# Agent attention and a SoLU feed-forward: the square of u without a bias column

## The chip, the cores and the metric

The kernel runs on one core of one Trainium2 chip. The metric is the device time of one execution in microseconds. Engines are named as in the profile: PE multiplies matrices (PEld loads its stationary operand), DVE is VectorE, ACT is ScalarE, POOL is GpSimd, SP issues the DMAs. Each runs its own list of instructions in order and waits on semaphores for the others.

## The reference, cut to what matters

```python
s = scale * (agents @ k.T); a2k = softmax(s); agent_v = a2k @ v
x = softmax(scale * (q @ agents.T)) @ agent_v       # 4 x 12608 tokens of 128
h = x @ w_in                                        # 128 -> 1024
e = exp(h - max(h)); sm = e / (sum(e) + 1e-9)
solu = h * sm
mu, var = mean(solu), mean((solu - mu) ** 2)
ln = (solu - mu) / sqrt(var + 1e-6) * g_ln
out = ln @ w_out                                    # 1024 -> 128
```

The kernel takes the mean of each column out of the scaled `w_out` beforehand, so the token's own mean is needed in the variance alone. It works with u = h * exp(h - max), not yet divided by the sum S of the exponentials; S then enters as a term that is added to the variance before the reciprocal root.

## The kernel before, in words

A tile is 128 tokens; there are 394. Each goes through the same steps.

- `c_h`: PE writes h into one of two PSUM buffers (`ph`).
- `c_max`: DVE writes -h and its row minimum to SBUF (`e_a`, `e_b`).
- `c_exp`: ACT writes the exponential back over `ph`, with the minimum as its bias column, and accumulates S.
- `c_u`: DVE multiplies the two into u (one of six buffers), and its accumulator gives the sum of u, in one of eight small tiles `su`.
- `c_sq`: ACT squares u. The function gets `-1024*u + su`, where `su` is the instruction's bias column, so the row sum of what it writes is the centred sum of squares, kept in a column of `Q`. The tile `sq` that it writes is read by nobody.
- For 11 of 13 tiles, `c_f0` and `c_f1` split u into two 16-bit parts (POOL, some of the first parts on ACT), `c_x` turns them by a transposing DMA, and `c_w` makes 24 matmuls. For the others PE transposes u itself (`c_t`, `c_ev`) and `c_w` makes 8 matmuls in fp32.

After a group of 16 tiles (8 at the ends, 2 in the last) `c_rstd` computes the reciprocal roots for the group: `t0` on ACT, `r2` on POOL (`t = Q + t`), two ACT functions (`y`), then four small POOL instructions up to `yc`. `c_fin` on DVE scales four tiles' results by `yc` on their way out of PSUM.

Between these lie the attention's first half for the next batch (`phase_a`) and the softmax over the agents for eight tiles at a time (`phase_b`).

The order of all instructions on all engines is written out beforehand: `STEPS` (lines 25 to 151) is a packed list of operations, and `Plan.run` issues them in that order. What stands in `op(...)` as a cost only decides which PSUM bank an operation takes.

Of the kernel before, what the change touches and what calls it, by code (L numbers as in the profile page):

```python
# [13 lines left out]
F32 = mybir.dt.float32  # L14
# [4 lines left out]
AF = mybir.ActivationFunctionType  # L19
ALU = mybir.AluOpType  # L20
# [146 lines left out]
class Plan:  # L167
# [17 lines left out]
    def op(self, eng, fn, cost, due, deps=(), take=False, free=None, after=(), kind=1, shy=0.0):  # L185
        o = Op()
        o.kind, o.shy = kind, shy
        o.eng, o.fn, o.cost, o.due, o.take, o.free = eng, fn, cost, due, take, free
        o.deps, o.outs, o.end, o.bank = [d for d in deps if d is not None], [], None, None
        o.left = 0  # L190
        self.ops.append(o)
        for d in o.deps + [d for d in after if d is not None]:
            if d.end is None:
                o.left += 1
                d.outs.append(o)
        return o
# [39 lines left out]
def kernel(  # L236
# [11 lines left out]
    nc = tc.nc  # L248
    B, C, N = kT.shape
    A = agT.shape[2]  # L250
    DF = w_in.shape[1]
    P = 128
# [3 lines left out]
    RT = 16  # L256
# [12 lines left out]
    UBUF = 6  # L269
# [73 lines left out]
    engs = (mybir.EngineType.PE, mybir.EngineType.Activation, mybir.EngineType.DVE, mybir.EngineType.Pool, mybir.EngineType.SP)  # L343
    SCALE = 1.0 / math.sqrt(C)
    INV = 1.0 / DF
    LIFT = DF ** 1.5

    const = ctx.enter_context(tc.tile_pool(name="const", bufs=1))
    mpool = ctx.enter_context(tc.tile_pool(name="mpool", bufs=2))
# [2 lines left out]
    tiny = ctx.enter_context(tc.tile_pool(name="tiny", bufs=4))  # L352
# [5 lines left out]
    ident = const.tile([P, P], F32, name="ident")  # L358
# [58 lines left out]
    def ring(m, shape, dt, name):  # L417
        return [const.tile(shape, dt, name=f"{name}_{chr(97 + i)}") for i in range(m)]

    pad = const.tile([P, 8], F32, name="pad")  # L420
    er, ur = ring(2, [P, DF], F32, "e"), ring(UBUF, [P, DF], F32, "u")
# [23 lines left out]
    def conv_out():  # L445
# [52 lines left out]
        def spread_ev():  # L498
            nc.vector.tensor_copy(out=wsc, in_=pm[0][:, :2])
            for i, k in enumerate((-0.5 * LIFT, 1.5 * LIFT)):  # L500
                nc.vector.tensor_scalar(out=lif[:, i : i + 1], in0=pm[0][:, 1:2], scalar1=k, scalar2=None, op0=ALU.mult)
# [39 lines left out]
    op = plan.op  # L541
# [11 lines left out]
    rgrp = {}  # L553
# [4 lines left out]
    def both(x):  # L558
        return seq[x][0] % 2 == 1 and seq[x][1] == 0

    sur, fcr = ring(8, [P, 1], F32, "su"), ring(12, [P, 1], F32, "fc")
    mxr, smr = ring(4, [P, UB], F32, "mx"), ring(4, [P, UB], F32, "sm")
    mdone, mlast, last_h, ex, CB, cbs = {}, {}, {}, {}, {}, {}
    bmats = {}
# [1 line left out]
    def phase_a(b, due, gate):  # L566
# [166 lines left out]
        def q5():  # L733
            cb, r = cbs[b], res["pr"]
            ri = r.bitcast(I32)
            nc.vector.tensor_scalar(out=ri[:, 1:2], in0=ri[:, 2:3], scalar1=0x7F800000, scalar2=None, op0=ALU.bitwise_and)
            k = math.sqrt(1e-6 * DF) * DF
            for i, z, f in ((1, 0, 2.0 ** 13 * k), (2, 0, 2.0 ** 13 * k * 1e-9), (3, 1, -(2.0 ** -14)), (4, 0, -(2.0 ** 13))):
                nc.vector.tensor_scalar(out=cb[:, i : i + 1], in0=r[:, z : z + 1], scalar1=float(f), scalar2=None, op0=ALU.mult)

# [40 lines left out]
        for c in range(NC):  # L781
# [3 lines left out]
            z = c * 2.55  # L785
# [16 lines left out]
        z = NC * 2.55 - (8.0 if head else 1.5)  # L802
# [10 lines left out]
        z = NC * 2.55 + 1.0  # L813
        fa = op("P", f1, 0.24, at(z), [AC[NCK], o7], take=True)
        fb = op(ETE, f2, (0.16, 0.2), at(z + 0.2), [fa] + mdone.get(b - 1, []))
        fc = op("D", q1, 0.2, at(z + 0.2), [fa], free=fa, after=[fb])
        fd = op("P", q2, 0.3, at(z + 0.4), [fc, wmax], take=True)
        fe = op("D", q3, 0.22, at(z + 0.5), [fd, OLD_CB.get(b - 2)], free=fd)
        CB[b] = op("D", q5, 0.33, at(z + 0.9), [fe])
        mdone[b] = []  # L820
        f4 = None
# [122 lines left out]
    us, phs, nms, nhs, rr, pr, st, fs, rs_ = {}, {}, {}, {}, {}, {}, {}, {}, {}  # L944
# [14 lines left out]
    def scal(x):  # L959
        return cbm[x] if both(x) else cbs[seq[x][0]]  # L960
# [25 lines left out]
    def c_exp(x):  # L986
        R, j = rgrp[x]
        if R not in rs_:
            rs_[R] = {z: tiny.tile([P, RT], F32, tag=z, name=f"{z}{R}") for z in "SQ"}
        nc.scalar.activation(out=phs[x], in_=nhs[x], func=AF.Exp, scale=-1.0, bias=nms[x], accum_out=rs_[R]["S"][:, j : j + 1])  # L990

    def xbar(x):
        return x % PEN not in PEP and x < n - TD

    def c_u(x):
        us[x] = (ur[x % UBUF], sur[x % 8])
        u, su = us[x]
        nc.vector.scalar_tensor_tensor(out=u, in0=nhs[x], scalar=scal(x)[:, 4:5], in1=phs[x],  # L998
                                       op0=ALU.mult, op1=ALU.mult, accum_out=su)

    def c_f0(x, k="G"):
        f = fs[x] = fr_[fl.index(x) % FBUF]
        if k == "A":
            nc.scalar.copy(out=f[:, 0, :], in_=us[x][0])
        else:
            nc.gpsimd.tensor_scalar(out=f[:, 0, :], in0=us[x][0], scalar1=1.0, scalar2=0.0, op0=ALU.mult, op1=ALU.add)

    def c_f1(x):
        nc.gpsimd.tensor_tensor(out=fs[x][:, 1, :], in0=us[x][0], in1=fs[x][:, 0, :], op=ALU.subtract)

    def c_x(x):
        pr[x] = xr[fl.index(x) % XB]
# [1 line left out]

    def c_sq(x):
        R, j = rgrp[x]
        u, su = us[x]
        sq = sqr[x % 2]
        nc.scalar.activation(out=sq, in_=u, func=AF.Square, bias=su, scale=-float(DF),  # L1019
                             accum_out=rs_[R]["Q"][:, j : j + 1])  # L1020

    def c_t(x, hf, pt):
        rr[x, hf] = pt
        for kf in range(4):
            k0 = hf * 4 + kf
            nc.tensor.transpose(pt[:, kf * P : (kf + 1) * P], us[x][0][:, k0 * P : (k0 + 1) * P], ident)  # L1026

    def c_ev(x, hf, k="A"):
        if hf == 0:
# [4 lines left out]
    def c_w(x, m0, m1, px=None):  # L1034
        G, j = divmod(x, GT)
        if px is not None:
            st[G] = {"po": px}
        po, t = st[G]["po"][:, j * P : (j + 1) * P], pr[x]
        mm = []
        for kf in range(NF):  # L1040
            if xbar(x):
                mm += [(t[:, kf, :], wh16, kf), (t[:, kf, :], wl16, kf), (t[:, NF + kf, :], wh16, kf)]
            else:
                mm.append((t[:, kf, :], w32, kf))
        for q in range(m0, m1):
            ut, wt, kf = mm[q]
            nc.tensor.matmul(po, ut, wt[:, kf, :], start=(q == 0), stop=(q == len(mm) - 1))  # L1047

    def c_rstd(R, m):
        gp = nc.gpsimd  # L1050

        def g(z):
            return rs_[R][z][:, :m]

        def t0():
            for z in ("t", "y", "z", "yc"):
                rs_[R][z] = tiny.tile([P, RT], F32, tag=z, name=f"{z}{R}")
            j0 = 0
            while j0 < m:
                c = scal(RS0[R] + j0)  # L1060
                j1 = next((j for j in range(j0, m) if scal(RS0[R] + j) is not c), m)
                nc.scalar.activation(out=rs_[R]["t"][:, j0:j1], in_=rs_[R]["S"][:, j0:j1], func=AF.Square,
                                     scale=c[:, 1:2], bias=c[:, 2:3])
                j0 = j1

        def r2():
            gp.tensor_tensor(out=g("t"), in0=g("Q"), in1=g("t"), op=ALU.add)

        def r3(z):
            if z == 0:  # L1070
                nc.scalar.activation(out=g("y"), in_=g("t"), func=AF.Ln, scale=float(2.0 ** -64))
            else:
                nc.scalar.activation(out=g("y"), in_=g("y"), func=AF.Exp, scale=-0.5, bias=lnb)

        def r4():
            gp.tensor_tensor(out=g("z"), in0=g("y"), in1=g("y"), op=ALU.mult)

        def r5():
            gp.tensor_tensor(out=g("z"), in0=g("z"), in1=g("t"), op=ALU.mult)

        def r6():
            gp.tensor_scalar(out=g("z"), in0=g("z"), scalar1=lif[:, :1], scalar2=lif[:, 1:2], op0=ALU.mult, op1=ALU.add)

        def r7():
            gp.tensor_tensor(out=g("yc"), in0=g("y"), in1=g("z"), op=ALU.mult)

        return t0, (("G", r2, 0.17), ("A", lambda: r3(0), 0.19), ("A", lambda: r3(1), 0.23), ("G", r4, 0.2), ("G", r5, 0.24), ("G", r6, 0.39), ("G", r7, 0.18))


# [10 lines left out]
    def F(f, *x):  # L1100
        return lambda *y: f(*x, *y)
# [45 lines left out]
    def at(x, d, r, l):  # L1147
        return x + d + (r * (1.0 - x / 12.0) if x < 12 else l if x >= X0[B - 1] else 0.0)

    H, MX, EX, U, SQ, T, EV, W, FIN, F0, F1, XT = ({} for _ in range(12))  # L1150
# [3 lines left out]
    for x in range(n):  # L1154
        b, t = seq[x]
        G, j = divmod(x, GT)
# [18 lines left out]
        used = [T.get((x - UBUF, 0)), T.get((x - UBUF, 1)), SQ.get(x - UBUF), F1.get(x - UBUF)]  # L1175
        U[x] = op("D", F(c_u, x), 1.205, at(x, DU_ + (0.0 if xbar(x) else DUF), DUR, DUL), [EX[x], CB[b]] + used + (cin if x < 2 else cout if x < UBUF else []), after=[U.get(x - 1)])
        SQ[x] = op("A", F(c_sq, x), 1.14, at(x, DSQ + (0.0 if xbar(x) else DSQF), DSQR, DSQL), [U[x]] + ([om] if not x else []))
        if xbar(x):
            fl.append(x)
# [20 lines left out]
        for m0 in range(0, num, step):  # L1200
            m1 = min(m0 + step, num)
            lead = m0 == 0 and j == 0
            f = (lambda px, x=x, m1=m1: c_w(x, 0, m1, px)) if lead else F(c_w, x, m0, m1)
# [93 lines left out]
```

## Time and profile before

| what | value |
| --- | --- |
| time, median of 3 runs | 1253.42 us (1252.56 to 1254.7) |
| span of the profiled execution | 1258.3 us |
| busy: PE, DVE, ACT, POOL | 97%, 95%, 94%, 89% of the span |
| squares of u on ACT (line 1019) | 394 |
| `r2` on POOL (line 1067) | 27 |

The profile gives the span of one execution, from the first to the last instruction, and no separate time for that execution; the span is 4.9 us over the median of the timed runs. Busy shares of four engines lie close together, so a single share names no bound: what decides is which engine is idle in which stretch, and for whom it waits. An ACT instruction with an accumulator shows as two rows, the function and a short ACTIVATION_READ_ACCUMULATOR.

### The profile page before, as it was taken

How to read it: one execution, taken by the hardware profiler on the slowest of the kernel's cores; microseconds unless marked ns; L12 is line 12 of the kernel's file. 1: busy time of each engine (PE TensorE's matmuls, PEld its weight loads, DVE VectorE, ACT ScalarE, POOL GpSimd, SP SyncE). 2: the span in 40 equal slices, each digit the busy share in tenths (PEclk: the TensorE clock that was granted, in tenths of full speed). 3: DMA queues.
4: the chain of work that ended last, by engine and by line, in shares of the span. 5: the costliest groups of instructions: out<-in, count | busy, mean ns of one | idle time of the engine just before them, and what ended most of it. 6: DMA issues, size and time to landing. Idle time of an engine off the chain costs nothing.

```text
span 1258.3 us, 36373 instructions
## 1 busy us (share of the span) xinstructions
PE 1214.6 (97%) x14304; PEld 936.6 (74%) x14304; DVE 1200.0 (95%) x2292; ACT 1183.8 (94%) x2212; POOL 1119.7 (89%) x889
## 2 busy tenths in 40 slices
PE   7989999999999999999999999999999999999998
PEld 4567777777777877777878777777787777777778
DVE  5799999999999999999999999899999999999997
ACT  5599999999999999999999999899999999999998
POOL 3488898999999898889999989789899999999995
PEclk8989999999999999999999999999999999999999
DMA  9599999999999999999999999999999899898896
GB/s 368 199 204 237 230 243 234 236 234 216 197 203 237 246 227 245 254 265 234 214 209 208 249 227 224 225 248 252 224 227 195 167 202 216 168 230 199 194 190 169
DMA packets 721516, 281.41 MB, mean 224 GB/s; under 512 B 692672, under 2 KB 696256, under 8 KB 721344
## 3 DMA queue, kind: packets, MB, share of 16 engines
q1 hardware_dynamic: 721344, 279.08, 103.2%
q8 instruction: 112, 1.84, 0.6%
q14 instruction: 60, 0.49, 0.1%
HBM read 79.67 MB, written 25.82 MB: 84 GB/s over the span
## 4 chain that ended last, share of the span: by engine, by line
ACT 24%; PE 24%; DVE 21%; issue 14%; POOL 9%; DMA 6%; SPq 0%; POOLq 0%; DVEq 0%; ACTq 0%
ACT ph L990 10%; PE px L1047 10%; PE ph L955 7%; ACT sq_b L1019 5%; ACT sq_a L1019 5%; DVE e_b L983 5%; DVE e_a L983 4%; PE px L654 2%; PE px L601 2%; DVE u_c L998 2%; DVE u_d L998 2%; DVE u_e L998 1%; DVE u_a L998 1%; PE px L1026 1%; DVE u_b L998 1%
## 5 line engine op out<-in xcount | busy, mean ns | idle before, releaser
L983 DVE TENSOR_SCALAR_CACHE_REDUCE e_a<-ph,nk 128x1024 f32<-128x1024 f32 x197 | 251.5, 1277 | 10.1 <-PE ph L955 9.2
L983 DVE TENSOR_SCALAR_CACHE_REDUCE e_b<-ph,nk 128x1024 f32<-128x1024 f32 x197 | 251.6, 1277 | 5.5 <-PE ph L955 5.0
L990 ACT ACTIVATE ph<-e_a,nm 128x1024 f32<-128x1024 f32 x197 | 219.3, 1113 | 16.3 <-DVE e_a L983 14.7
L990 ACT ACTIVATE ph<-e_b,nm 128x1024 f32<-128x1024 f32 x197 | 219.3, 1113 | 9.6 <-DVE e_b L983 8.4
L998 DVE SCALAR_TENSOR_TENSOR u_d<-e_b,cb,ph 128x1024 f32<-128x1024 f32 x66 | 84.2, 1276 | 2.2 <-ACT ph L990 1.9
L998 DVE SCALAR_TENSOR_TENSOR u_a<-e_a,cb,ph 128x1024 f32<-128x1024 f32 x66 | 84.1, 1275 | 1.8 <-ACT ph L990 1.4
L998 DVE SCALAR_TENSOR_TENSOR u_c<-e_a,cb,ph 128x1024 f32<-128x1024 f32 x65 | 82.8, 1274 | 2.3 <-ACT ph L990 1.3
L998 DVE SCALAR_TENSOR_TENSOR u_e<-e_a,cb,ph 128x1024 f32<-128x1024 f32 x65 | 82.8, 1274 | 1.6 <-ACT ph L990 1.1
L998 DVE SCALAR_TENSOR_TENSOR u_b<-e_b,cb,ph 128x1024 f32<-128x1024 f32 x65 | 82.9, 1276 | 1.2 <-ACT ph L990 0.6
L998 DVE SCALAR_TENSOR_TENSOR u_f<-e_b,cb,ph 128x1024 f32<-128x1024 f32 x65 | 82.7, 1273 | 1.3 <-ACT ph L990 0.7
L1047 PE MATMUL px<-wh,x_c 128*128 128x128 f16 x672 | 71.4, 220 | 2.6 <-DMA x_c<-f_e 2.3
L1047 PE MATMUL px<-wh,x_b 128*128 128x128 f16 x672 | 71.5, 219 | 1.1 <-DMA x_b<-f_a 0.7
L1047 PEld LDWEIGHTS <-x_b 128*128 128x128 f16 x1008 | 61.4, 98 | 14.8 <-issue 5.7
L1047 PEld LDWEIGHTS <-x_c 128*128 128x128 f16 x1008 | 62.4, 98 | 13.3 <-DMA x_c<-f_e 3.1
L1047 PE MATMUL px<-wh,x_a 128*128 128x128 f16 x672 | 70.1, 219 | 2.0 <-DMA x_a<-f_c 1.3
L1047 PEld LDWEIGHTS <-x_d 128*128 128x128 f16 x984 | 61.1, 99 | 14.3 <-issue 2.8
L1047 PEld LDWEIGHTS <-x_a 128*128 128x128 f16 x1008 | 61.7, 98 | 12.7 <-DMA x_a<-f_c 1.9
L1047 PE MATMUL px<-wh,x_d 128*128 128x128 f16 x656 | 69.5, 220 | 1.5 <-DVE u_c L998 0.7
L1047 PE MATMUL px<-wh,x_h 128*128 128x128 f16 x656 | 69.3, 219 | 1.7 <-DMA x_h<-f_c 1.3
L1047 PEld LDWEIGHTS <-x_h 128*128 128x128 f16 x984 | 60.5, 98 | 13.7 <-DMA x_h<-f_c 1.5
L1047 PEld LDWEIGHTS <-x_e 128*128 128x128 f16 x984 | 60.2, 98 | 13.2 <-issue 3.8
L1047 PE MATMUL px<-wh,x_g 128*128 128x128 f16 x656 | 68.5, 219 | 1.0 <-DMA x_g<-f_e 1.0
(457 smaller groups left out, 4733.3 us busy)
## 6 DMA issues: line engine op xcount, KB each, us to landing
qt_a<-in_qT_dram SPq DMA_DIRECT2D x24, 512.0 KB, 5.1
qt_b<-in_qT_dram SPq DMA_DIRECT2D x24, 512.0 KB, 5.2
out_dram<-ob_a SPq DMA_DIRECT2D x24, 512.0 KB, 3.7
out_dram<-ob_b SPq DMA_DIRECT2D x24, 512.0 KB, 3.6
kt_b<-in_kT_dram SPq DMA_DIRECT2D x18, 512.0 KB, 4.7
vt_b<-in_v_dram SPq DMA_DIRECT2D x18, 512.0 KB, 4.9
kt_a<-in_kT_dram SPq DMA_DIRECT2D x18, 512.0 KB, 5.0
vt_a<-in_v_dram SPq DMA_DIRECT2D x18, 512.0 KB, 4.8
```

The lines of the kernel that those rows point to most:

```text
L601: nc.tensor.matmul(px[h * AP2 : (h + 1) * AP2, :w], ag_sb[:, b, :], kt[:, o : o + w], start=True, stop=True)
L654: nc.tensor.matmul(px[h * AP2 : (h + 1) * AP2, :C], eT[:w, o + h * AP2 : o + (h + 1) * AP2], vt[:w, t, :], start=all(z[0] != h for z in mm ...
L955: nc.tensor.matmul(ph[:, sl], w, m[:, sl], start=(q == 0), stop=(q == len(mm) - 1))
L983: nc.vector.tensor_scalar(out=nhs[x], in0=phs[x], scalar1=nks[k][:, j : j + 1], scalar2=None, op0=ALU.mult, op1=ALU.min, accum_out=nms[x])
L990: nc.scalar.activation(out=phs[x], in_=nhs[x], func=AF.Exp, scale=-1.0, bias=nms[x], accum_out=rs_[R]["S"][:, j : j + 1])
L998: nc.vector.scalar_tensor_tensor(out=u, in0=nhs[x], scalar=scal(x)[:, 4:5], in1=phs[x], op0=ALU.mult, op1=ALU.mult, accum_out=su)
L1019: nc.scalar.activation(out=sq, in_=u, func=AF.Square, bias=su, scale=-float(DF), accum_out=rs_[R]["Q"][:, j : j + 1])
L1026: nc.tensor.transpose(pt[:, kf * P : (kf + 1) * P], us[x][0][:, k0 * P : (k0 + 1) * P], ident)
L1047: nc.tensor.matmul(po, ut, wt[:, kf, :], start=(q == 0), stop=(q == len(mm) - 1))
```

## The change

ACT's square no longer has the bias column: it squares `32*u`, and its accumulator gives 1024 times the raw sum of squares. The sum of u goes to a column of a new tile `U` of the group. On POOL, `r2` gets three instructions ahead of the old one, once for each group: U*U, Q - U*U, and the maximum with zero. The constants of `t0` and of the lift are rescaled to match. `STEPS` is the same.

```diff
-    LIFT = DF ** 1.5
+    LIFT = float(DF)
+    RN = DF ** 0.5
...
-            k = math.sqrt(1e-6 * DF) * DF
+            k = 1e-3 * DF
...
-            rs_[R] = {z: tiny.tile([P, RT], F32, tag=z, name=f"{z}{R}") for z in "SQ"}
+            rs_[R] = {z: tiny.tile([P, RT], F32, tag=z, name=f"{z}{R}") for z in "SQU"}
...
-        us[x] = (ur[x % UBUF], sur[x % 8])
-        u, su = us[x]
+        R, j = rgrp[x]
+        u = us[x] = ur[x % UBUF]
         nc.vector.scalar_tensor_tensor(out=u, in0=nhs[x], scalar=scal(x)[:, 4:5], in1=phs[x],
-                                       op0=ALU.mult, op1=ALU.mult, accum_out=su)
+                                       op0=ALU.mult, op1=ALU.mult, accum_out=rs_[R]["U"][:, j : j + 1])
...
-        nc.scalar.activation(out=sq, in_=u, func=AF.Square, bias=su, scale=-float(DF),
-                             accum_out=rs_[R]["Q"][:, j : j + 1])
+        nc.scalar.activation(out=sq, in_=us[x], func=AF.Square, scale=RN, accum_out=rs_[R]["Q"][:, j : j + 1])
...
         def r2():
+            gp.tensor_tensor(out=g("U"), in0=g("U"), in1=g("U"), op=ALU.mult)
+            gp.tensor_tensor(out=g("Q"), in0=g("Q"), in1=g("U"), op=ALU.subtract)
+            gp.tensor_scalar(out=g("Q"), in0=g("Q"), scalar1=0.0, scalar2=None, op0=ALU.max)
             gp.tensor_tensor(out=g("t"), in0=g("Q"), in1=g("t"), op=ALU.add)
```

On PE, DVE, ACT and SP every instruction stands where it stood. Only POOL's list grows. Its rows in the middle of the program, at a group of 16 tiles (about 532 us in the trace of before), were these; `f_d` and `f_e` are the 16-bit parts, and what stands in brackets is whom the instruction waits for:

```order
L1009 TENSOR_TENSOR f_d<-u_c,f_d 128x1024 [waits Pool_49]
L1067 TENSOR_TENSOR t_6555<-Q_5868,t_6555 128x16 [waits Activation_49]
L1076 TENSOR_TENSOR z_6557<-y_6556 128x16 [waits Activation_49]
L1079 TENSOR_TENSOR z_6557<-z_6557,t_6555 128x16 [waits Pool_49]
L1082 TENSOR_SCALAR z_6557<-z_6557,lif 128x16 [waits Pool_49]
```

The same place of the changed kernel, whose line numbers are two or three higher there:

```order
L1010 TENSOR_TENSOR f_d<-u_c,f_d 128x1024 [waits Pool_49]
L1066 TENSOR_TENSOR U_5890<-U_5890 128x16 [waits DVE_49]
L1067 TENSOR_TENSOR Q_5889<-Q_5889,U_5890 128x16 [waits Activation_49,Pool_49]
L1068 TENSOR_SCALAR Q_5889<-Q_5889 128x16 [waits Pool_49]
L1069 TENSOR_TENSOR t_6580<-Q_5889,t_6580 128x16 [waits Pool_49]
L1078 TENSOR_TENSOR z_6582<-y_6581 128x16 [waits Activation_49]
L1081 TENSOR_TENSOR z_6582<-z_6582,t_6580 128x16 [waits Pool_49]
```

Three instructions stand ahead of the sum into `t`, each waiting for the one before; the wait for ACT's square has moved to the second of them.

The last rows of POOL's list before, where the group of 2 tiles comes between the parts of a group of 8:

```order
L1082 TENSOR_SCALAR z_17428<-z_17428,lif 128x8 [waits Pool_49]
L1067 TENSOR_TENSOR t_17543<-Q_17405,t_17543 128x2 [waits Activation_49]
L1085 TENSOR_TENSOR yc_17429<-y_17427,z_17428 128x8
L1076 TENSOR_TENSOR z_17545<-y_17544 128x2 [waits Activation_49]
L1079 TENSOR_TENSOR z_17545<-z_17545,t_17543 128x2 [waits Pool_49]
```

And in the changed kernel:

```order
L1084 TENSOR_SCALAR z_17522<-z_17522,lif 128x8 [waits Pool_49]
L1066 TENSOR_TENSOR U_17499<-U_17499 128x2 [waits DVE_49]
L1067 TENSOR_TENSOR Q_17498<-Q_17498,U_17499 128x2 [waits Activation_49,Pool_49]
L1068 TENSOR_SCALAR Q_17498<-Q_17498 128x2 [waits Pool_49]
L1069 TENSOR_TENSOR t_17640<-Q_17498,t_17640 128x2 [waits Pool_49]
L1087 TENSOR_TENSOR yc_17523<-y_17521,z_17522 128x8
L1078 TENSOR_TENSOR z_17642<-y_17641 128x2 [waits Activation_49]
```

Here the three new ones stand ahead of `yc` of the group before as well.

## Rows read from the trace of the kernel before

**Rows 1.** The page, part 1: busy us (share of the span) xinstructions.
```profile
PE 1214.6 (97%) x14304; PEld 936.6 (74%) x14304; DVE 1200.0 (95%) x2292; ACT 1183.8 (94%) x2212; POOL 1119.7 (89%) x889
```

**Rows 2.** Three stretches: length, busy us of PE, PEld, DVE, ACT, POOL (instructions).
```profile
90.00:1000.00 910.00, 893.94 (x10692) 693.62 (x10690) 885.82 (x1692) 873.97 (x1641) 832.69 (x648) 1.00 1.09 228
1000.00:1230.00 230.00, 218.99 (x2594) 172.78 (x2593) 227.21 (x406) 228.28 (x410) 225.06 (x172) 1.00 0.97 199
1230.00:1258.00 28.00, 25.03 (x292) 22.38 (x291) 20.02 (x35) 22.24 (x42) 13.58 (x20) 0.98 0.65 170
```

**Rows 3.** Waits: who waited for whom, us in total, times, longest.
```profile
ACT ph L990 <- DVE e_a L983: 14.7, 23, 2.0
DVE e_a L983 <- PE ph L955: 9.2, 11, 3.7
...
DVE u_d L998 <- ACT ph L990: 1.9, 6, 0.6
```

**Rows 4.** Chain of waits, shares by line: 90:1000 us, 1000:1258, and 1230:1258.
```profile
by line: issue 13.1%; PE px L1047 13.1%; ACT ph L990 8.9%; PE ph L955 8.7%; DVE e_b L983 4.7%; ACT sq_b L1019 4.2%; DVE e_a L983 4.2%; ACT sq_a L1019 4.0%; DVE u_c L998 1.8%; PE px L1026 1.7%; PE px L654 1.7%; DVE u_e L998 1.6%; DVE u_d L99
...
by line: issue 21.0%; ACT ph L990 16.8%; ACT sq_b L1019 7.7%; ACT sq_a L1019 7.3%; DVE e_a L983 4.4%; DVE e_b L983 4.1%; POOL f_a L1009 3.3%; POOL f_b L1009 2.5%; POOL f_c L1009 2.5%; DVE u_d L998 2.1%; DVE u_a L998 2.0%; POOL f_e L1009 1.7
...
by line: ACT ph L990 21.0%; ACT sq_b L1019 19.6%; issue 12.9%; ACT sq_a L1019 12.1%; DVE e_b L983 5.2%; DVE u_a L998 4.6%; PE px L1047 2.6%; ACT y L1073 2.2%; DVE ob_b L1092 2.1%; ACT t L1062 2.0%; ACT t_e L1031 1.7%; POOL z L1082 1.2%; ACT
```

**Rows 5.** Groups of instructions on ACT: count, busy us, mean ns, idle before.
```profile
L1019 ACT ACTIVATE sq_a<-u_a,su_a 128x1024 bf16<-128x1024 f32 x17 | 19.4, 1144 | 0.1
...
L1019 ACT ACTIVATE sq_b<-u_f,su_b 128x1024 bf16<-128x1024 f32 x16 | 18.2, 1136 | 0.0
...
L1073 ACT ACTIVATE y<-y,lnb 128x16 f32<-128x16 f32 x23 | 7.1, 308 | 0.7
...
L1071 ACT ACTIVATE y<-t 128x16 f32<-128x16 f32 x23 | 4.8, 207 | 1.2 <-POOL t L1067 1.1
...
L1004 ACT CAST f_d<-u_e 128x1024 f16<-128x1024 f32 x3 | 3.1, 1041 | 0.2 <-DVE u_e L998 0.2
```

**Rows 6.** ACT in order of time: start us, us, instruction.
```profile
317.64 0.67 ACT L750 ACTIVATE mh<-px,cb 128x512 f16<-128x512 f32 x1
318.20 0.56 ACT L1031 COPY t_e<-px 128x512 f32<-128x512 f32 x1
318.67 1.15 ACT L1019 ACTIVATE sq_a<-u_e,su_c 128x1024 bf16<-128x1024 f32 x1
```

**Rows 7.** Line 1067 on POOL: durations (ns), and who waited for it.
```profile
L1067 POOL TENSOR_TENSOR t<-Q,t x27: 194/220/234, 86.9 to 1251.8; 128x16 f32<-128x16 f32 x23, 128x8 f32<-128x8 f32 x3, 128x2 f32<-128x2 f32 x1
...
  ACT y L1071: 1.4, 4
```

**Rows 8.** One group at 190 us in order of time, ACT's row first, then POOL's.
```profile
190.48 0.22 ACT L1071 ACTIVATE y<-t 128x16 f32<-128x16 f32 x1
...
190.23 0.22 POOL L1067 TENSOR_TENSOR t<-Q,t 128x16 f32<-128x16 f32 x1 [0.94 <-ACT sq_a L1019]
191.12 0.21 POOL L1076 TENSOR_TENSOR z<-y 128x16 f32<-128x16 f32 x1 [0.67 <-ACT y L1073]
191.41 0.22 POOL L1079 TENSOR_TENSOR z<-z,t 128x16 f32<-128x16 f32 x1
191.74 0.35 POOL L1082 TENSOR_SCALAR z<-z,lif 128x16 f32<-128x16 f32 x1
192.18 0.22 POOL L1085 TENSOR_TENSOR yc<-y,z 128x16 f32<-128x16 f32 x1
```

**Rows 9.** Pieces of the chain of waits with line 1067: first, one of POOL's run, last.
```profile
141.72 0.22 POOL t L1067
...
1116.20 0.18 POOL t L1067
...
1251.80 0.20 POOL t L1067
```

**Rows 10.** DVE at the end, in order of time.
```profile
1254.41 0.29 DVE L1092 TENSOR_TENSOR ob_b<-px,yc 128x128 f32<-128x128 f32 x1 [0.95 <-POOL yc L1085]
```

More of the change, by code (lines that the diff above doesn't have):

```diff
@@ L559, in both @@
         return seq[x][0] % 2 == 1 and seq[x][1] == 0
-    sur, fcr = ring(8, [P, 1], F32, "su"), ring(12, [P, 1], F32, "fc")
+    fcr = ring(12, [P, 1], F32, "fc")
     mxr, smr = ring(4, [P, UB], F32, "mx"), ring(4, [P, UB], F32, "sm")
@@ L1003, in c_f0 @@
         if k == "A":
-            nc.scalar.copy(out=f[:, 0, :], in_=us[x][0])
+            nc.scalar.copy(out=f[:, 0, :], in_=us[x])
         else:
-            nc.gpsimd.tensor_scalar(out=f[:, 0, :], in0=us[x][0], scalar1=1.0, scalar2=0.0, op0=ALU.mult, op1=ALU.add)
+            nc.gpsimd.tensor_scalar(out=f[:, 0, :], in0=us[x], scalar1=1.0, scalar2=0.0, op0=ALU.mult, op1=ALU.add)
     def c_f1(x):
-        nc.gpsimd.tensor_tensor(out=fs[x][:, 1, :], in0=us[x][0], in1=fs[x][:, 0, :], op=ALU.subtract)
+        nc.gpsimd.tensor_tensor(out=fs[x][:, 1, :], in0=us[x], in1=fs[x][:, 0, :], op=ALU.subtract)
     def c_x(x):
@@ L1016, in c_sq @@
         R, j = rgrp[x]
-        u, su = us[x]
         sq = sqr[x % 2]
-        nc.scalar.activation(out=sq, in_=u, func=AF.Square, bias=su, scale=-float(DF),
-                             accum_out=rs_[R]["Q"][:, j : j + 1])
+        nc.scalar.activation(out=sq, in_=us[x], func=AF.Square, scale=RN, accum_out=rs_[R]["Q"][:, j : j + 1])
     def c_t(x, hf, pt):
@@ L1025, in c_t @@
             k0 = hf * 4 + kf
-            nc.tensor.transpose(pt[:, kf * P : (kf + 1) * P], us[x][0][:, k0 * P : (k0 + 1) * P], ident)
+            nc.tensor.transpose(pt[:, kf * P : (kf + 1) * P], us[x][:, k0 * P : (k0 + 1) * P], ident)
     def c_ev(x, hf, k="A"):
```

## The prediction

> **What bounds the kernel now.** I read the busy shares first, then busy time by stretch, the waits, the chain of waits, and last the rows of the instructions that change. The busy shares lie between 89% and 97% [rows 1], so no engine is the bound by itself. By stretch there is more to see [rows 2]. What a stretch has beyond an engine's busy time is idle: from 90 to 1000 us DVE is idle for 24 of 910 us (910 - 885.8), ACT for 36, POOL for 77. From 1000 to 1230 us, where the attention's first half has no further batch to prepare, ACT is idle for 1.7 of 230 us, DVE for 2.8 and POOL for 4.9: three engines are full at once. The last 28 us are a tail in which things wait for each other.
>
> The waits say how the engines hang together [rows 3]. ACT's longest wait is for DVE's row minimum (14.7 us), DVE's is for PE's h (9.2 us), and of ACT's exponential DVE waits little (1.9 us in the largest of six such groups). So ACT is seldom the one for whom DVE is idle directly; it holds things up in a loop (minimum, exponential, u, next h), whose parts stand in line on their engines. The chain of waits shows how much of it is squares [rows 4]: 4.2 + 4.0 = 8.2% of the first stretch, and 7.7 + 7.3 = 15.0% of the last 258 us. That is 910 x 0.082 = 74.6 us and 258 x 0.150 = 38.7 us; at 1.14 us each, 65 and 34 of the 394 squares. The others lie beside work of other engines.
>
> **The square without its column.** The 24 groups of squares have means from 1136 to 1144 ns or a little over (the first and the last group in [rows 5]), and I take 1.14 us. The trace has no square without a column, so its cost is bounded by rows. A cast of the same 1024 elements from SBUF to 16 bits in SBUF, which has no column, takes 1041 ns: 0.10 us less. Two functions on the same tile of 16 columns, one with a bias column and one without, take 308 and 207 ns: again 0.10 us [rows 5]. In start to start, a scaling of 512 elements by a column takes 318.20 - 317.64 = 0.56 us and a plain copy of 512 elements takes 318.67 - 318.20 = 0.47 us: 0.09 us, so the column costs engine time and not only a longer row [rows 6]. The low end is 0, if the accumulator's read sets the pace of these instructions; the high end is 0.10. I take 0.10 us, to which two of the three pairs point: 394 x 0.10 = 39 us less work on ACT.
>
> The Trainium skill (ScalarE: Activation LUTs, What ACT_TABLE_LOAD costs) gives about 93 ns for each pointer operand, and also says that ACTIVATEs back to back overlap by about 93 ns. By the price alone ACT would lose an estimated 394 x 0.093 = 37 us; had the operand's cost lain in that overlap, it would lose nothing. The trace decides for the first: the pair above differs by 0.09 us from start to start.
>
> On the chain that is 65 x 0.10 = 6.5 us before 1000 us and 34 x 0.10 = 3.4 us behind it, of which the tail has about 8 squares (32% of its 28 us by the third row) and so 0.8.
>
> **The three new instructions on POOL.** Each group of 16 tiles has them ahead of its `t`, and there are 27 groups [rows 7]. The trace has no such instruction at this place, but it has a chain of four small ones that wait for each other [rows 8]: from start to start 191.41 - 191.12 = 0.29 us, 0.33 and 0.44 (the last behind a tensor-scalar with two columns, 0.35 us long; the new one has one constant). Three of them cost between 3 x 0.22 = 0.66 us (durations alone, row of line 1067) and 3 x 0.44 = 1.3; I take 0.33 each, 1.0 us. That makes 27 us more work on POOL, which hides in its idle time before 1000 us (19 groups or so in 77 us), and hardly behind it: six groups there, 6 us against 4.9 idle.
>
> The group's own path gets longer too. Where POOL already stands waiting for the last square, as at 190 us (0.94 us idle), the first of the three runs inside that wait, and `t` comes 0.66 us later; elsewhere 1.0. Behind `t` on ACT stands the logarithm of line 1071, and everything that ACT has behind it waits with it. At 190 us it began 0.03 us behind the end of `t` [rows 8]; ACT waited for `t` in 4 groups so far, 1.4 us in all [rows 7], and it will in many more. Part of that comes out of ACT's 39 us. On the chain of waits line 1067 stands in six places that pass the delay on, counted in the pieces of the chain (the first, one in which POOL is simply busy, and the last stand in [rows 9]): four behind a square (0.66 us each) and two in a run of POOL (1.0 each), 4.6 us in all. One of the four is the end of the program: the group of two tiles has nothing behind which its path could hide, and DVE waits there for `yc` already, 0.95 us [rows 10].
>
> The other edits cost nothing: DVE's accumulator writes to another column with the same instruction, the constants only change value, and the tile `U` is used again four groups later, long after POOL read it.
>
> **The sum.** Before 1000 us: 6.5 us less, of which I keep three quarters, 4.9. A chain that gets shorter is not the longest any more at some places; DVE is next there, and its 24 us of idle time, mostly behind PE, are all that could close. POOL's three places there, 3 x 0.66 = 2.0 more. From 1000 to 1230 us: squares 2.6 less, POOL's two places 2.0 more, and DVE and POOL are full, so 0.6 less at most; I count 0. The tail: 0.8 less, 0.66 more, so 0.1 less. Together 4.9 - 2.0 + 0.1 = 3.0 us less: a span of 1255.3 instead of 1258.3. The profile has only the span, 4.9 us over the median of the timed runs; I take the same 3.0 us off the median: 1253.4 - 3.0 = 1250.4.
>
> **Rivals.** (1) *DVE takes over at once.* ACT is done earlier and waits longer for the row minimum, already its longest wait [rows 3]; the time stays within 2.5 us of 1253.4. For it speaks that DVE is 97 to 99% busy between 90 and 1230 us; against it that a tenth of the chain is squares.
>
> (2) *POOL becomes the bound, and it gets slower.* The place is the stretch from 1000 us on, the only one where POOL has no room. There six groups at 1.0 us come to 6 us, the squares' gain ends at DVE (2.8 us of idle time), and with POOL late the split tiles reach the transposing DMA and then PE later. 6.0 more there, less 2.9 before 1000 us and 0.1 in the tail: 3.0 us more, 1256.4. It decides once POOL's idle time there is used up, that is above 0.8 us for each group (4.9 / 6); my price lies over that point, but part of POOL's wait for squares is idle time in which the new work fits, and an engine that is ahead by some tiles can give a microsecond away.
>
> (3) *More comes out.* ACT's whole schedule of 394 squares loosens, and DVE's idle time closes by a third: 27 us idle from 90 to 1230 us make 9 us less, 1244.4. Against it: DVE waits for PE more than for ACT.
>
> (4) *The column was free* since the accumulator's read sets the pace. Then only POOL's 4.6 us are left: 1258.0. The start-to-start pair speaks against it [rows 6].
>
> **How the numbers follow.** What a measurement of this kernel can tell from no change is about 0.2%, 2.5 us. Chances: my forecast, 2.5 to 6 us less, 0.41; rival 1, 0.33; rival 2, 0.14; rival 3, 0.09; rival 4, 0.03. So faster 0.50 (forecast and rival 3), same 0.33, slower 0.17. The range reaches from near rival 3 to rival 2: 1245.0 to 1256.5. The likeliest case's own range is 1247.4 to 1250.9.
>
> **What would show it.** The squares' mean is 1.04 us, and ACT's busy time falls by 35 to 39 us while DVE's and PE's stay. POOL's grows by 18 to 27 us, with idle time from 1000 us on near nothing. ACT's wait for `t` at line 1071's place grows from 1.4 us to 8 or more and its wait for DVE's row minimum above the 14.7 us. The squares' share of the chain falls. I am wrong on the price if the squares stay above 1.1 us; wrong on the coupling if DVE's idle time falls by more than 6 us; wrong on POOL if waits of PE for `x` grow, or POOL stays under 97% busy from 1000 us on.

## The result, and the profile after

The changed kernel takes 1260.09 us (median of 9 runs, 1257.89 to 1265.86) against 1254.7 us of the kernel before on the same occasion (9 runs, 1250.75 to 1258.41): a ratio of 1.0052 [1.0031, 1.0073]. It is slower by half a percent, on the other side of what was forecast, and above the range. A second measurement beside other kernels gave 1261.72 against 1255.48, 1.0045 [1.003, 1.0061].

The profiled span is 1258.3 us for both kernels, which is an accident. A timed run is about 1.8 us longer than its span (1260.09 against 1258.3), so by that estimate the profiled execution of before took 1260.1 us, more than any of its nine runs here. Spans of single profiles are therefore not compared below: kernels are compared by ratios within one occasion, places by stretches of the same tiles. "Stretch 312 to 393" is the time from the start of exponential number 312 on ACT to the last one, number 393. It lies where the order has no further batch to prepare, and where the instructions from there on are the same it repeats to 1.5 us (230.02, 231.39 and 231.49 in three executions, 225.23 and 225.19 in two others). The stretch from 48 to 312 moves by several us between executions (802.16 and 808.14 with the same instructions).

The page of the kernel after, busy time and share of each engine, and the chain of waits by engine; they answer to [rows 1]:

```profile
PE 1212.5 (96%) x14304; PEld 936.5 (74%) x14304; DVE 1199.9 (95%) x2292; ACT 1159.2 (92%) x2212; POOL 1136.3 (90%) x970
...
PE 34%; POOL 23%; DVE 16%; issue 15%; DMA 6%; ACT 5%; SPq 1%; POOLq 0%; DVEq 0%; ACTq 0%
```

The chain of before went 24% through ACT and 9% through POOL; now it goes 5% through ACT and 23% through POOL. The squares have left the path and POOL has come into it. POOL has 81 instructions more (27 groups by 3). The page has DVE and PE as busy as before to within a few us.

Busy time of PE, PEld, DVE, ACT and POOL in the two stretches, as in [rows 2]:

```profile
90.00:1000.00 910.00, 894.47 (x10692) 694.64 (x10691) 885.73 (x1693) 856.20 (x1640) 845.49 (x701) 1.00 1.09 228
1000.00:1230.00 230.00, 215.91 (x2568) 170.38 (x2567) 223.79 (x401) 220.62 (x404) 225.96 (x188) 1.00 0.94 197
```

From 1000 us on, the order has changed: ACT was busiest there with 228.28 us and is now at 220.62; DVE fell from 227.21 to 223.79, so that it idles for 6.2 us instead of 2.8; POOL alone rose, from 225.06 to 225.96. DVE and ACT both have room now and the kernel is slower.

The chain of waits of after by line, from 1000 us to the end, as in the second line of [rows 4]:

```profile
by line: issue 23.4%; POOL f_a L1010 7.1%; POOL f_b L1010 7.0%; POOL f_d L1010 4.8%; ACT ph L991 4.6%; POOL f_e L1010 4.5%; POOL f_c L1010 4.2%; POOL f_a L1007 3.6%; POOL f_e L1007 3.3%; DVE e_b L984 3.3%; POOL f_b L1007 3.2%; POOL f_d L100
```

The eight groups of POOL's splits that the line shows whole come to 37.7%. The squares, 7.7% and 7.3% before, are not among what it shows, and so are under 3.2% each.

The squares after, two of their six groups (count, busy us, mean ns, idle before), answering to [rows 5]:

```profile
L1019 ACT ACTIVATE sq_a<-u_a 128x1024 bf16<-128x1024 f32 x66 | 69.3, 1049 | 0.3
...
L1019 ACT ACTIVATE sq_a<-u_e 128x1024 bf16<-128x1024 f32 x65 | 68.3, 1051 | 1.0 <-DVE u_e L999 0.8
```

The mean went from 1136 to 1144 ns to 1048 to 1051 ns.

The new instructions on POOL and the one behind them (durations in ns: least, median, most), answering to [rows 7]:

```profile
L1066 POOL TENSOR_TENSOR U<-U x27: 194/215/252, 84.1 to 1251.0; 128x16 f32<-128x16 f32 x23, 128x8 f32<-128x8 f32 x3, 128x2 f32<-128x2 f32 x1
L1067 POOL TENSOR_TENSOR Q<-Q,U x27: 195/221/225, 84.6 to 1251.3; 128x16 f32<-128x16 f32 x23, 128x8 f32<-128x8 f32 x3, 128x2 f32<-128x2 f32 x1
L1068 POOL TENSOR_SCALAR Q<-Q x27: 215/244/248, 84.9 to 1251.6; 128x16 f32<-128x16 f32 x23, 128x8 f32<-128x8 f32 x3, 128x2 f32<-128x2 f32 x1
L1069 POOL TENSOR_TENSOR t<-Q,t x27: 195/220/223, 85.2 to 1251.9; 128x16 f32<-128x16 f32 x23, 128x8 f32<-128x8 f32 x3, 128x2 f32<-128x2 f32 x1
```

And the waits of after (us in total, times, longest), as in [rows 3]:

```profile
ACT ph L991 <- DVE e_a L984: 22.4, 39, 3.8
...
ACT y L1073 <- POOL t L1069: 12.7, 18, 1.6
...
DVE e_a L984 <- PE ph L956: 7.1, 10, 2.6
...
DVE ob_b L1094 <- POOL yc L1087: 4.9, 9, 0.9
...
PEld L905 <- POOL pack L898: 4.3, 3, 2.9
```

ACT waits for `t` in 18 groups instead of 4, and longer for the row minimum (14.7 us before). The last two lines are what matters most below: other engines than ACT wait for POOL (1.3 us for `yc` and 1.9 for `pack` before).

### The profile page after: what moved, and what is told of

It is laid out like the page before. It is cut to its first block, busy times and chain, and to the rows that moved or that the text cites. A ratio compares the mean times of both kernels' runs of the same rounds, so it can differ in the third digit from the quotient of the medians.

```text
span 1258.3 us, 36484 instructions
## 1 busy us (share of the span) xinstructions
PE 1212.5 (96%) x14304; PEld 936.5 (74%) x14304; DVE 1199.9 (95%) x2292; ACT 1159.2 (92%) x2212; POOL 1136.3 (90%) x970
## 4 chain that ended last, share of the span: by engine, by line
PE 34%; POOL 23%; DVE 16%; issue 15%; DMA 6%; ACT 5%; SPq 1%; POOLq 0%; DVEq 0%; ACTq 0%
PE px L1046 15%; PE ph L956 10%; DVE e_b L984 4%; DVE e_a L984 3%; POOL f_a L1010 3%; POOL f_b L1010 3%; PE px L655 3%; ACT ph L991 3%; POOL f_d L1010 2%; POOL f_e L1010 2%; POOL f_c L1010 2%; POOL f_e L1007 2%; PE px L602 2%; POOL f_b L1007 2%; POOL f_c L1007 2%
## 5 line engine op out<-in xcount | busy, mean ns | idle before, releaser
L991 ACT ACTIVATE ph<-e_a,nm 128x1024 f32<-128x1024 f32 x197 | 219.7, 1115 | 25.1 <-DVE e_a L984 22.4
L1046 PE MATMUL px<-wh,x_e 128*128 128x128 f16 x656 | 68.9, 219 | 1.9 <-DMA x_e<-f_a 1.4
L1046 PEld LDWEIGHTS <-x_c 128*128 128x128 f16 x1008 | 62.0, 98 | 11.4 <-issue 2.2
L1019 ACT ACTIVATE sq_a<-u_c 128x1024 bf16<-128x1024 f32 x66 | 69.2, 1048 | 1.0 <-DVE u_c L999 0.7
L1019 ACT ACTIVATE sq_b<-u_b 128x1024 bf16<-128x1024 f32 x66 | 69.2, 1049 | 0.9 <-DVE u_b L999 0.5
```

What stands on the lines that cost most here:

```text
L1019: nc.scalar.activation(out=sq, in_=us[x], func=AF.Square, scale=RN, accum_out=rs_[R]["Q"][:, j : j + 1])
```

## The experiments

The experiments were to tell three theories apart. **A**: the price is on the group's own path, since the three instructions stand ahead of `t` and ACT waits for it; behind `t` they would cost little. **B**: the price is POOL's time wherever the instructions stand, since POOL has no room from 1000 us on. **C**: the cheaper square itself gains nothing, or loses, as its gain ends at DVE. All ratios are against the kernel before, run on the same occasion; kernels of different occasions are compared by these ratios, and a difference of two ratios has the two intervals' half-widths added in squares.

**The square alone.** The changed kernel without the three lines, so that the square of the mean isn't subtracted:

```diff
-            gp.tensor_tensor(out=g("U"), in0=g("U"), in1=g("U"), op=ALU.mult)
-            gp.tensor_tensor(out=g("Q"), in0=g("Q"), in1=g("U"), op=ALU.subtract)
-            gp.tensor_scalar(out=g("Q"), in0=g("Q"), scalar1=0.0, scalar2=None, op0=ALU.max)
```

> The changed kernel without its three new POOL instructions in r2; the square of the sum is not subtracted, so the variance term is left out. ACT has the cheap squares, POOL what it had before. Theory A (the longer way from the last square of a group to ACT's logarithm costs the time): ratio to before 0.995 to 0.998, and ACT's wait for t back at about 1.4 us. Theory B (POOL's time itself costs): the same, 0.995 to 0.998. Theory C (an ACT that runs ahead of the written order collides with other work, whatever POOL does): 1.002 to 1.006.

Measured: 1253.73 against 1260.59, 0.9956 [0.9935, 0.9977], or 5.5 us less. C falls. All of the loss, 1.0045 - 0.9956 = 0.89% (plus or minus 0.26), about 11 us, comes with the three small instructions.

**The three instructions alone, ahead of `t` and behind it.** Three of the same kind and size in the kernel before, with its bias column; they compute U = S - S, Q = Q - U and max(Q, 0), which changes nothing in Q:

```diff
+            gp.tensor_tensor(out=g("U"), in0=g("S"), in1=g("S"), op=ALU.subtract)
+            gp.tensor_tensor(out=g("Q"), in0=g("Q"), in1=g("U"), op=ALU.subtract)
+            gp.tensor_scalar(out=g("Q"), in0=g("Q"), scalar1=0.0, scalar2=None, op0=ALU.max)
             gp.tensor_tensor(out=g("t"), in0=g("Q"), in1=g("t"), op=ALU.add)
```

> The kernel before, with the square's bias column, and three more POOL instructions of the same kind and the same waits in r2 ahead of t; they change no value (S - S, Q - 0, maximum with 0). Theory A: 1.006 to 1.010, about 27 x (0.66 to 1.0) us of delay of which a third to a half shows. Theory B: 1.004 to 1.010. Theory C: 0.998 to 1.003.

> The kernel before with the same three POOL instructions, but behind t, so that nothing waits for them except POOL's own next instructions. Theory A: 0.999 to 1.002. Theory B: as with the three ahead of t, 1.004 to 1.010. Theory C: 0.998 to 1.003.

Measured: 1263.36, 1.0032 [1.0005, 1.006], ahead of `t`; 1263.38, 1.0024 [1.0, 1.0048], behind it. The place makes no difference that shows, and both cost less than half of the 0.89%. Neither A nor B had this in its ranges. It looks as if ACT with its dear squares covered part of POOL's new work; the traces of the last stretch, below, don't bear that out.

**Both, with the three behind `t`.** The changed kernel with its `t` moved ahead of the three lines, so that the square of the mean comes too late to count:

```diff
+            gp.tensor_tensor(out=g("t"), in0=g("Q"), in1=g("t"), op=ALU.add)
             gp.tensor_tensor(out=g("U"), in0=g("U"), in1=g("U"), op=ALU.mult)
             ...
-            gp.tensor_tensor(out=g("t"), in0=g("Q"), in1=g("t"), op=ALU.add)
```

> The changed kernel with its three POOL instructions behind t instead of ahead of it; what they compute is then not used, so the square of the sum is left out of the variance. ACT's squares are cheap, POOL is loaded, the path to the logarithm is as short as before. Theory A: 0.995 to 0.999. Theory B: 1.003 to 1.006, like the changed kernel. Theory C: 1.002 to 1.006.

Measured: 1261.2, 1.0012 [0.9991, 1.0032]. ACT's wait for `t` is short again:

```profile
ACT y L1073 <- POOL t L1066: 3.0, 6, 0.7
```

3.0 us instead of 12.7, yet the instructions still cost 1.0012 - 0.9956 = 0.56% (plus or minus 0.29). So A is not the main thing: off the path they cost over half of what they do on it, though less than B had. The rest, 1.0045 - 1.0012 = 0.33% (plus or minus 0.26), can be the path's; in stretch 312 to 393 it doesn't show (230.61 us behind `t`, 230.02 to 231.49 ahead of it).

**Again, and fewer.** The changed kernel a second time (1.0045, above), then two instructions before the last square has come, without the max:

```diff
-            gp.tensor_tensor(out=g("Q"), in0=g("Q"), in1=g("U"), op=ALU.subtract)
-            gp.tensor_scalar(out=g("Q"), in0=g("Q"), scalar1=0.0, scalar2=None, op0=ALU.max)
+            gp.tensor_tensor(out=g("t"), in0=g("t"), in1=g("U"), op=ALU.subtract)
```

and then only this subtraction on POOL, with the square of U on ACT, ahead of the group's last square (again without the max):

```diff
+        if x == n - 1 or rgrp[x + 1][1] == 0:
+            q2 = rs_[R]["U"][:, : j + 1]
+            nc.scalar.activation(out=q2, in_=q2, func=AF.Square)
...
-            gp.tensor_tensor(out=g("U"), in0=g("U"), in1=g("U"), op=ALU.mult)
-            gp.tensor_tensor(out=g("Q"), in0=g("Q"), in1=g("U"), op=ALU.subtract)
-            gp.tensor_scalar(out=g("Q"), in0=g("Q"), scalar1=0.0, scalar2=None, op0=ALU.max)
+            gp.tensor_tensor(out=g("t"), in0=g("t"), in1=g("U"), op=ALU.subtract)
```

> The changed kernel itself once more, beside the next three on one chip. If the two parts of the change add up as the first four runs have them (square 0.9956; three instructions 1.0024 to 1.0056): 0.998 to 1.002. If there is more to it when they come together, because the logarithm then waits longer on an ACT that is ahead: 1.003 to 1.007, as measured first.

> The same result by two POOL instructions instead of three, none of them behind the last square: U = U*U and t = t - U run ahead of the wait, then t = Q + t as before; no maximum with zero. Theory of POOL's load (each instruction costs about 0.19% of the time, wherever it stands): 0.998 to 1.001. Theory of the path (only what stands between the last square and t costs): 0.995 to 0.997, like the square alone.

> The square of U is made on ACT, ahead of the group's last square of u (27 small ACT instructions), and POOL has one new instruction, t = t - U, ahead of its wait. Theory of POOL's load: 0.996 to 0.999. Theory of the path: 0.995 to 0.997.

Measured: with two 1256.03, 1.001 [0.999, 1.0029]; with one 1251.28, 0.996 [0.9941, 0.9978], against 0.9956 with none. More instructions cost more, though not evenly: +0.04%, +0.54%, +0.89% (plus or minus 0.28 or so each) for one, two, three. In stretch 312 to 393 the steps are more even: 1.1, 2.8 and 4.8 to 6.3 us over the square alone. The two early ones stand off the path and still cost 0.54%: A's range is missed, B's is met. With one on POOL the change is worth making: it beats the kernel before by 0.4%, and the changed kernel of the same occasion by 10 us.

**Which groups cost.** The three lines only in the first 19 groups, or only in the last 8 (the other groups leave out the square of the mean):

```diff
+            if R < 19:      # the other kernel: if R >= 19:
                 gp.tensor_tensor(out=g("U"), in0=g("U"), in1=g("U"), op=ALU.mult)
                 ...
```

> The changed kernel with the three POOL instructions in the first 19 groups only (up to about 1000 us); in the last 8 the square of the sum is left out of the variance. If the loss comes from the stretch in which POOL is full (from 1000 us on): 0.995 to 0.998, nearly the square alone. If it comes from all groups alike: within 0.003 of the changed kernel on the same chip, and at least 0.003 above the square alone (0.9986 or more).

> The changed kernel with the three POOL instructions in the last 8 groups only; in the first 19 the square of the sum is left out of the variance. If the two parts of the loss add up (changed kernel 1.0045, first 19 groups alone 0.9991, none 0.9956): 1.000 to 1.003. If nearly all of the loss lies in the last stretch: 1.003 to 1.005.

Measured: the first 19 alone 1255.1, 0.9991 [0.9965, 1.0016], that is 0.35% (plus or minus 0.33) over none; the last 8 alone 1260.08, 1.0011 [0.9988, 1.0034], 0.55% (plus or minus 0.31) over none. The two parts add up; the first 19 alone meet neither of their ranges. In us that is 4.4 for 19 groups, 0.23 each, and 6.9 for 8, 0.86 each. The stretch 312 to 393 shows the same without the timed runs' scatter. Its length and each engine's busy time, for the square alone, then for the last 8 groups, then for the changed kernel's second execution and its first:

```profile
1013.00:1238.30 225.30, 216.13 (x2579) 172.39 (x2577) 222.23 (x397) 220.07 (x403) 218.05 (x169) 1.00 0.94 197
```
```profile
1017.90:1249.40 231.50, 218.25 (x2577) 173.69 (x2575) 222.73 (x396) 220.39 (x403) 222.19 (x188) 0.99 0.92 192
```
```profile
1019.60:1251.00 231.40, 218.21 (x2577) 173.44 (x2575) 222.80 (x396) 220.39 (x403) 222.07 (x188) 0.99 0.90 192
```
```profile
1016.00:1246.00 230.00, 216.76 (x2578) 172.41 (x2576) 222.62 (x396) 220.32 (x402) 222.08 (x188) 1.00 0.92 192
```

It takes 225.3 us without the new instructions, 231.5 with them in the last groups, 231.4 and 230.0 with them in all, and 225.19 with them in the first groups alone; 227.24 in the kernel before and 226.30 with one on POOL. Six groups have their `t` in this stretch, so the 4.8 to 6.3 us are 0.8 to 1.0 us each. In the second execution DVE's idle time grows from 3.1 to 8.6 us, as much as the stretch does but for 0.6: DVE stood next to being the bound and now waits. POOL is even a little less full in percent (222.07 of 231.4, and 218.05 of 225.3): it acts as a list in a fixed order that others wait for, not as a sum of work that overflows.

The three instructions alone, ahead of `t` in the kernel with the dear squares, have this in the same stretch:

```profile
1017.60:1249.70 232.10, 219.02 (x2581) 173.69 (x2579) 223.24 (x397) 225.37 (x403) 222.04 (x188) 0.99 0.92 192
```

That is 4.9 us over the 227.24 of the kernel before (and 2.8 with the three behind `t`). So here they cost as much beside dear squares as beside cheap ones, within the 1.5 us by which the stretch repeats. The chain of waits from 1000 us on agrees, first for the square alone, then for the three instructions beside dear squares:

```profile
by line: issue 31.5%; DVE e_b L984 10.2%; DVE e_a L984 8.8%; ACT ph L991 7.6%; DVE u_e L999 4.7%; DVE u_a L999 4.3%; ACT sq_b L1019 2.7%; DVE u_b L999 2.6%; ACT sq_a L1019 2.1%; DVE u_f L999 1.9%; DVE u_c L999 1.9%; DVE u_d L999 1.8%; POOL 
```
```profile
by line: issue 21.9%; POOL f_b L1009 7.4%; POOL f_a L1009 7.4%; ACT ph L990 5.4%; POOL f_d L1009 4.7%; POOL f_e L1009 4.4%; POOL f_c L1009 4.2%; POOL f_a L1006 3.6%; POOL f_c L1006 3.2%; POOL f_b L1006 3.2%; POOL f_d L1006 3.2%; ACT sq_b L1
```

Cheaper squares alone put DVE on the chain. In these traces POOL comes onto it with its new instructions, also where ACT's squares are dear.

**Where one of the delays passes through.** Start, length and instruction at one place (idle time and releaser in brackets), first without the new instructions, then with them (second execution of the changed kernel):

```profile
1213.80 1.04 POOL L1007 TENSOR_SCALAR f_e<-u_f 128x1024 f16<-128x1024 f32 x1
1214.81 0.20 POOL L1066 TENSOR_TENSOR t<-Q,t 128x8 f32<-128x8 f32 x1
...
1217.37 0.47 POOL L898 TENSOR_TENSOR pack<-logits,pack 128x147 f16<-128x147 f32 x1
1217.89 0.34 PE L905 MATMUL px<-ident,pack 128*128 128x128 f16 x3 [0.42 <-POOL pack L898]
1219.47 1.28 DVE L984 TENSOR_SCALAR_CACHE_REDUCE e_a<-ph,nk 128x1024 f32<-128x1024 f32 x1 [0.59 <-PE ph L956]
```
```profile
1224.23 1.04 POOL L1007 TENSOR_SCALAR f_e<-u_f 128x1024 f16<-128x1024 f32 x1
1225.24 0.20 POOL L1066 TENSOR_TENSOR U<-U 128x8 f32<-128x8 f32 x1
...
1226.13 0.20 POOL L1069 TENSOR_TENSOR t<-Q,t 128x8 f32<-128x8 f32 x1
...
1228.68 0.46 POOL L898 TENSOR_TENSOR pack<-logits,pack 128x147 f16<-128x147 f32 x1
1229.19 0.34 PE L905 MATMUL px<-ident,pack 128*128 128x128 f16 x3 [2.42 <-POOL pack L898]
1231.42 1.28 DVE L984 TENSOR_SCALAR_CACHE_REDUCE e_a<-ph,nk 128x1024 f32<-128x1024 f32 x1 [3.25 <-PE ph L956]
```

`t` starts 0.89 us behind the first new instruction, and 0.88 us more lie between `f_e` and `pack` (4.45 us against 3.57 from start to start). But PE waits 2.42 us instead of 0.42 for `pack`, and DVE 3.25 instead of 0.59 for the h behind it: here POOL arrives with a backlog of about 2 us, gathered over groups before, and hands it on at once. Counted from exponential 312, POOL's large instructions start 0.8, 1.8, 2.5, 3.0 and 3.9 us later than in the square alone behind the first five groups, and `pack`, behind the sixth, 4.7; ACT's exponentials are only 2.7 us later up to number 384. Line 905 is the transposes of the finished logits; POOL's small work for them stands behind the splits in POOL's list. The three instructions beside dear squares pass their delay on at the same place, where PE had not waited in the kernel before:

```profile
1227.48 0.50 PE L904 MATMUL px<-ident,pack 128*128 128x128 f16 x3 [2.21 <-POOL pack L897]
```

Smaller steps of the same kind stand earlier in the second execution of the changed kernel, where `t` or `yc` is late:

```profile
1030.64 0.69 DVE L1094 TENSOR_TENSOR ob_b<-px,yc 128x512 f32<-128x512 f32 x1 [0.42 <-POOL yc L1087]
...
1075.24 0.21 ACT L1073 ACTIVATE y<-t 128x16 f32<-128x16 f32 x1 [1.03 <-POOL t L1069]
...
1076.96 1.28 DVE L999 SCALAR_TENSOR_TENSOR u_c<-e_a,cb,ph 128x1024 f32<-128x1024 f32 x1 [0.68 <-ACT ph L991]
```

In the second of them ACT waits 1.03 us for `t`, the next exponential is late, and DVE waits 0.68 us for it: the path's part.

**Taking work off POOL there.** If POOL's lateness is the cause, seven of its casts of 1.04 us, moved to ACT from tile 312 on, should give the time back to the changed kernel but not to the others:

```diff
-                    args.append(e)
+                    args.append("A" if e == "G" and any(o is z for z in self.flip[::8]) else e)
...
+        if x >= 312:
+            plan.flip.append(F0[x])
```

> The changed kernel with 7 of the first 16-bit parts (about 1.05 us each on POOL) made by ACT instead, all behind tile 312; the order is the same. It takes as much from POOL there as the new instructions gave it (8 groups at about 0.9 us). If POOL is what the last stretch stands on: 0.998 to 1.001, that is 0.004 to 0.006 below the changed kernel, and tile 312 to the last exponential takes 225 to 227 us instead of 230 to 231. If the loss there has another cause (the path to the logarithm, or the order that no longer fits): 1.003 to 1.006, as the changed kernel.

> The version with the square of U on ACT and one instruction on POOL, with the same 7 parts moved to ACT. If POOL bounds the last stretch there too: 0.993 to 0.996, up to 2 us below the version without the move. If DVE is the bound by then: the same as without, 0.995 to 0.997.

> The kernel before with the same 7 parts moved to ACT. There ACT was idle for 1.7 us only from 1000 to 1230 us, so 6.6 us more on it should cost: 1.002 to 1.005. If POOL alone was the bound there already: 0.996 to 0.999.

Measured: the changed kernel with it 1260.78, 1.0027 [1.0002, 1.0051]; one on POOL with it 1258.78, 0.9985 [0.9962, 1.0007]; the kernel before with it 1265.03, 1.0048 [1.0027, 1.0069]. Stretch 312 to 393 of the changed kernel with it:

```profile
1021.50:1251.90 230.40, 217.38 (x2577) 172.40 (x2575) 222.77 (x396) 225.17 (x408) 215.58 (x181) 1.00 0.92 193
```

POOL has 6.5 us less to do than in the 231.4 us above, but the stretch is only 1 us shorter, and not 4 or more as B expected: ACT's seven casts cost elsewhere. For the kernel before they make the stretch longer by 6.2 us (227.24 to 233.44), for one on POOL by 3.7 (226.30 to 230.03), for the changed kernel by between -0.9 and +0.5 (231.39 and 230.01 to 230.47). So the move was worth 3 to 7 us more to the changed kernel than to the others, as B wants, but ACT's idle time in this stretch would give such an order by itself: 2.2 us in the kernel before, 5.7 with one on POOL, 9.7 to 11.0 in the changed kernel. As a test of the ratio it is inconclusive: 1.0027 lies between the two ranges and its interval overlaps that of 1.0045. One on POOL with the move, 0.9985, misses both of its ranges; the kernel before with it meets the first, ACT's cost. The step at `pack` (above, 2 to 2.6 us) shrank to 0.4 us in it.

## Why the prediction was wrong

**Right: the square.** A price of 0.10 us was taken and 0.093 measured (means of all 394 squares: 1141.3 to 1048.8 ns). The Trainium skill (ScalarE: Activation LUTs, What ACT_TABLE_LOAD costs) gives about 93 ns for a pointer operand, and the trace agrees. The gain by itself was put at 4.9 us before 1000 us, 2.6 up to 1230 us (all but 0.6 of it given to POOL) and 0.8 in the tail; the square alone gave 5.5 us (plus or minus 2.6), of which the stretch 312 to 393 has 2.0 (227.24 to 225.23). Whether the quarter taken off before 1000 us was the right size can't be told from these. Rivals 3 and 4 fall with the size of the gain and the price, and rival 1 with a loss of more than 2.5 us.

**Right: the waits.** ACT's wait for `t` was to rise from 1.4 us to 8 or more (12.7), that for the row minimum above 14.7 (22.4; 24.9 in the square alone, so it comes with the cheaper square), and the squares' share of the chain to fall. POOL's busy time was to grow by 18 to 27 us and grew by 16.6, a little under the range. Neither sign that was set for being wrong on POOL came, though the prediction was: POOL is 98.2% busy from 1000 us on (225.96 of 230), and PE's waits for `x` moved both ways (9.1 us in all before, 7.1 and 11.4 in two executions after). PE waited for `pack`, which no sign watched.

**Half right: ACT's busy time.** It was to fall by 35 to 39 us and fell from 1183.8 to 1159.2, by 25. The durations of all its rows add up to about 1358 us before and 1322 after, the forecast 36 less; but rows overlap and busy time counts an overlap once. The overlap fell from 174 to 163 us, so part of the shorter rows had been covered by others already.

**Wrong: POOL's instructions.** This is the step that failed. The prediction put them on the path at six places, 4.6 us, of which 2.0 from 1000 to 1230 us, set this against the squares' 2.6 and counted 0. They cost about 11 us: 4.4 us in the first 19 groups (with an interval that goes down to nearly nothing) where 2.0 was forecast, and 6.9 in the last 8 where 2.0 and 0.66 were; the stretch 312 to 393 alone has 4.8 to 6.3. The price of one group was not the error: 1.0 us was taken, and `pack` is 4.7 us later behind six groups, 0.8 each. The error was to count only the places where line 1067 stood on *before's* chain, two from 1000 to 1230 us, and to give the other four groups there no cost. POOL's list keeps most of the delay of every group, and where another engine needs one of its late entries, as PE needs `pack`, the backlog is handed on. The cheaper squares aren't needed for that: beside dear squares the same stretch grows by 4.9 us.

Over the whole program relief and load do hang together by the timed runs: the three instructions cost 0.32% ahead of `t` where ACT keeps its dear squares and 0.89% where it doesn't, a difference of 0.57% (plus or minus 0.38). That ACT's relief lays POOL's load bare is one reading of this, but the last stretch doesn't show it, and no trace places the difference.

**Rival 2 came nearest.** It named the place (from 1000 us on), the price (six groups by 1.0 us) and that POOL's lateness reaches PE; it was given 0.14. Its way, through the transposing DMA, is not the one that the traces show: PE waits for `pack`. Its point of decision, POOL's 4.9 us of idle time against 6 of new work, had been passed by its own numbers; the prediction talked itself out of it with idle time in which the work might fit. In fact POOL's idle time wasn't used up: between small instructions that wait for each other it idles too (0.29 us from start to start for a row of 0.20 or 0.22), and it has 7.9 to 9.3 us of idle time in the stretch now. Its 3.0 us more fall short of the 5.6 to 6.5 measured; it took 2.0 us for the first 19 groups, where the runs have 4.4.

**The tail.** One delay of 0.66 us was forecast at the end of the program. With the last group:

```profile
1251.01 0.19 POOL L1066 TENSOR_TENSOR U<-U 128x2 f32<-128x2 f32 x1
...
1251.87 0.20 POOL L1069 TENSOR_TENSOR t<-Q,t 128x2 f32<-128x2 f32 x1
1252.09 0.20 ACT L1073 ACTIVATE y<-t 128x2 f32<-128x2 f32 x1 [1.02 <-POOL t L1069]
...
1254.43 0.29 DVE L1094 TENSOR_TENSOR ob_b<-px,yc 128x128 f32<-128x128 f32 x1 [0.89 <-POOL yc L1087]
```

`t` starts 0.86 us behind the first of the three, and ACT waits 1.02 us for it with nothing else to do. Yet the end does not come later: from exponential 393 to the last instruction it is 12.31 us in the square alone and 12.29 and 12.39 in two executions with the three. In the square alone the last `yc` is ready 1.2 us before DVE uses it, so this delay has room there. The term of 0.66 us measured nothing to 0.1. The squares' 0.8 us less in the tail does not show either: from exponential 388 to the end it is 29.85 us before and 29.79 in the square alone.

**What stays open.** How the first 19 groups' 0.35% divides between path and backlog, and where the 0.57% lies that the three instructions cost less beside dear squares: the stretch from 48 to 312 took 806.85 us before, 807.26 and 809.43 in two executions of the changed kernel, and 802.16 for the square alone, which is too much scatter to place single microseconds. Whether an order worked out anew for the cheaper squares would hide three instructions was not tried. And POOL's share of the chain isn't by itself a price: with one instruction on POOL its splits fill the chain from 1000 us on just as much, and that kernel is the faster one. The chain names the engine that is waited for; what that costs took the runs.

## What to carry to other kernels

Where an engine works through a fixed list with 2% to spare, price new work on it by every group that carries it, not by the places where its line stands on the old chain, and look for the point at which another engine needs a late entry of that list. Here one, two and three small instructions cost 0.2, 0.5 and 0.8 to 1.0 us for each group in the last stretch. A change made of a gain and a payment is worth splitting: here the gain was kept by moving part of the payment's arithmetic to the engine that was relieved and leaving the maximum out (one instruction on POOL, 0.996 [0.9941, 0.9978]).

## What was not expected of the hardware

- Three instructions on 128x16 elements, each of which needs the one before, delay the fourth by 0.85 to 0.94 us on POOL where nothing else is waited for in between, while their rows last 0.215, 0.221 and 0.244 us (0.68 in all). The rest, some 0.2 us for each group, is in no busy figure.
- An engine's busy time can fall by less than the work taken from it: 36 us less in ACT's rows gave 25 us less busy time.
- 81 instructions of about 0.22 us, 1.5% of POOL's busy time, cost 0.89% of the whole, on an engine that the page shows at 89% busy.
